# Two token tiles' transposes in a PSUM bank each, emptied in pieces of 128 columns, at the head of a gated attention kernel

## The chip, the cores and the metric

One core of a Trainium2 chip. The metric is the device time of one execution, in microseconds (us). The profiled execution gives a span that is shorter than the time of the same execution (470.1 against 471.88 for the kernel before).

## The reference

Two attention blocks read the same `x` (2048 tokens, 1024 wide) and are mixed by a gate. Only the first projection of block A matters here, the keys:

```python
qkv = (x @ wqkv)...            # A: linear attention; B: sliding, dilated window of 8
q, k, v = qkv[0], qkv[1], qkv[2]
...
x = A_x
g = sigmoid((x * gate_w).sum(-1, keepdims=True))
return g * A(x) + (1 - g) * B(x)
```

## The kernel before

TensorE multiplies `x` by the key weights with `x` transposed: the kernel hands it both operands with the contraction over the 1024 columns along partitions. Most of `x` is transposed by DMA. That path is slow to start: the first such transfer is issued at 1.83 us and lands at 7.31, where the first plain rows, issued at 0.80, land at 3.81. So the first 256 columns (K-slices 0 and 1, of 128 columns each) of token tiles 0 to 3 come in as plain rows, and TensorE transposes them itself into PSUM, the memory that its results go to. PSUM is cut into banks; each tile of the two pools below is one bank.

```python
with tc.manual_schedule(engines={SP, mybir.EngineType.Activation}):
    for kt in range(2):                                   # key weights, slices 0 and 1, 128 KB each
        nc.scalar.dma_start(out=WkA[0][:, kt, :], in_=A_wqkv[kt * P:(kt + 1) * P, D:D + 512])
    load_wk(nc.scalar, 0, 1)                              # slices 0 and 1 of the other half, 256 KB
    load_rows(nc.sync, 0, 2, 0, 2 * P)                    # rows of tiles 0 and 1, 128 KB
    load_rows(nc.sync, 2, 4, 0, 2 * P)                    # rows of tiles 2 and 3
    load_xT(1, 0, 4)                                      # from here on transposed by DMA
    load_wk(nc.sync, 1, 0)
    ...
# ps_pj and ps_1: two PSUM pools of four banks each
def project(pj, t, kt, half):
    nc.tensor.matmul(pj[:], lhsT=xT[:, kt, t * P:(t + 1) * P], rhs=WkA[half][:, kt, :],
                     start=(kt == 0), stop=(kt == KT - 1))

warm_up(26)                                               # 26 matmuls of ones, results unused
def transpose_rows(t):
    for kt in range(2):
        xt = ps_1.tile([P, 2 * P], BF16, name="xt_ps", tag="p1")       # one bank, two tiles
        for i in range(2):
            nc.tensor.transpose(xt[:, i * P:(i + 1) * P], xrow[:, t + i, kt * P:(kt + 1) * P], ident)
        (nc.scalar.copy if kt else nc.vector.tensor_copy)(out=xT[:, kt, t * P:(t + 2) * P], in_=xt[:])

transpose_rows(0)
first = [bank_k(i) for i in range(4)]
for t in range(2):
    project(first[t], t, 0, 0)
transpose_rows(2)
first += [bank_k(i) for i in range(4, 8)]
for t in range(2):
    project(first[t], t, 1, 0)
for half, ts in ((0, (2, 3)), (1, range(4))):
    ...                                                   # then TensorE runs on without a break
```

In the profile a transpose writes `xt_ps`, a copy reads it into `xT`, and a projection writes `pk_ps`.

The softmax here doesn't subtract the row's maximum and nothing guards it: scores larger than these inputs give would overflow.

## Time and profile before

| | kernel before |
|---|---|
| time, median of 3 runs | 472.62 us (472.1 to 472.7) |
| TensorE busy | 466.2 of 470.1 us |
| rows of tile 0 landed | 3.81 us |
| first projection starts | 4.60 us |

The prediction shows the lines behind this table. In them "[0.27 <-DVE xT L211]" means that the engine sat idle for 0.27 us, until the VectorE copy of line 211 let it go. PE is the stream of matmuls and PEld that of weight loads, which run ahead of the matmuls (the load at 4.83 us is for the matmul at 5.04). The ends of matmuls in a profile are modelled, not measured. Idle time of PEld is therefore no loss by itself.

### The profile page before, as it was taken

Reading aid. Unit: us, or ns where it says so; the run is one execution under the profiler, and the core shown is the slowest. Engines: PE = TensorE matmul, PEld = TensorE weight load, DVE = VectorE, ACT = ScalarE, POOL = GpSimd, SP = SyncE. Lnnn points to the kernel's source line nnn. Section 1 sums busy time; section 2 is a strip of 40 time slices with the busy share of each in tenths; the row PEclk is TensorE's granted clock in tenths of the full one; section 3 lists DMA queues with packets and bytes.
Section 4 is the critical chain, followed back from the end, with each engine's and each line's share of the span. In section 5 each row is a group of like instructions: output and inputs, shape, how many; then the busy total and the mean of one; then the engine's idle time right before and its main releaser. Section 6 shows DMA issues by size and latency. Waiting matters only on the chain.

```text
span 470.1 us, 13202 instructions
## 1 busy us (share of the span) xinstructions
PE 466.2 (99%) x5762; PEld 265.9 (57%) x5762; DVE 278.1 (59%) x612; ACT 169.6 (36%) x277; POOL 15.7 (3%) x30
## 2 busy tenths in 40 slices
PE   8999999999999999999999999999999999999997
PEld 5444444445444444444888888888764444444444
DVE  2586689990219999999566676667660049800000
ACT  1443311112433333335465555555543134221121
POOL 2500001400000000000000000000000000000000
PEclk9999999999999999999999999999999999999999
DMA  9999960000653233627326523533763923221111
GB/s 235 201 244 371 349 212 0 0 1 1 226 130 117 83 141 123 162 93 251 105 55 106 116 59 73 88 80 82 92 165 76 216 75 79 68 56 45 34 33 46
DMA packets 98188, 55.14 MB, mean 117 GB/s; under 512 B 69074, under 2 KB 90578, under 8 KB 98130
## 3 DMA queue, kind: packets, MB, share of 16 engines
q1 hardware_dynamic: 92818, 49.61, 41.3%
q10 hardware_dynamic: 5312, 4.69, 3.1%
q8 instruction: 45, 0.74, 0.7%
q14 instruction: 13, 0.11, 0.1%
HBM read 26.10 MB, written 15.86 MB: 89 GB/s over the span
## 4 chain that ended last, share of the span: by engine, by line
PE 99%; DMA 1%; DVE 0%; issue 0%; DVEq 0%
PE q_ps L421 26%; PE d_ps L627 12%; PE p_ps L325 12%; PE pk_ps L196 12%; PE g_ps L264 12%; PE e_ps L627 12%; PE p_ps L361 9%; PE po L501 2%; PE s2b L479 2%; DMA xrow<-in_A_x_dram 1%; PE kv_ps L284 0%; PE w_ps L180 0%; PE xt_ps L210 0%; DVE osb L634 0%; DVE xT L211 0%
## 5 line engine op out<-in xcount | busy, mean ns | idle before, releaser
L421 PE MATMUL q_ps<-xT,WqB 64*64 64x512 bf16 x1024 | 70.2, 376 | 0.0
L421 PE MATMUL q_ps<-xT,WkB 64*64 64x512 bf16 x1024 | 69.8, 376 | 0.0
L171 DVE TENSOR_SCALAR e<-e 128x512 f32<-128x512 f32 x64 | 27.2, 424 | 62.0 <-ACT e L170 61.9
L325 PE MATMUL p_ps<-WvB,xT 128*128 128x512 bf16 x256 | 57.4, 379 | 0.0
L196 PE MATMUL pk_ps<-WkA,xT 128*128 128x512 bf16 x256 | 55.6, 379 | 0.3 <-DVE xT L211 0.3
L264 PE MATMUL g_ps<-pk,xrow 128*128 128x512 bf16 x256 | 55.4, 379 | 0.0
L484 ACT ACTIVATE PT<-s2b 128x928 bf16<-128x928 f32 (+4 forms) x40 | 34.2, 855 | 50.2 <-PE s2b L479 49.2
L486 DVE TENSOR_TENSOR PT<-PT,mask 128x928 bf16<-128x928 bf16 (+4 forms) x40 | 23.6, 589 | 36.5 <-ACT PT L484 36.5
L421 PEld LDWEIGHTS <-WkB 64*64 64x64 bf16 x1024 | 39.7, 107 | 7.3 <-DMA vd<-tmp 0.2
L361 PE MATMUL p_ps<-WqA,xT 128*128 128x512 bf16 x192 | 43.4, 379 | 0.0
L627 PEld LDWEIGHTS <-pqT 128*128 128x128 bf16 x272 | 26.0, 98 | 29.6 <-issue 0.2
L627 PEld LDWEIGHTS <-OBT 128*128 128x128 bf16 x272 | 26.0, 98 | 29.4
L264 PEld LDWEIGHTS <-xrow 128*128 128x128 bf16 x256 | 25.0, 98 | 30.2
L421 PEld LDWEIGHTS <-WqB 64*64 64x64 bf16 x1024 | 38.6, 107 | 6.1 <-DVE qz L461 0.2
L196 PEld LDWEIGHTS <-xT 128*128 128x128 bf16 x256 | 24.8, 98 | 30.3 <-DVE xT L211 0.8
L325 PEld LDWEIGHTS <-xT 128*128 128x128 bf16 x256 | 24.9, 98 | 30.2 <-issue 0.5
L634 DVE TENSOR_SCALAR osb<-e_ps,omg 128x128 bf16<-128x128 f32 x1 | 0.4, 351 | 57.3 <-PE e_ps L627 57.3
L330 ACT CAST tmp<-p_ps 128x512 bf16<-128x512 f32 x32 | 18.7, 587 | 37.9 <-PE p_ps L325 32.5
L501 PEld LDWEIGHTS <-PT 64*56 64x56 bf16 (+2 forms) x1152 | 29.1, 104 | 5.5
L170 ACT ACTIVATE e<-pk_ps 128x512 f32<-128x512 f32 x32 | 18.9, 597 | 36.2 <-PE pk_ps L196 32.5
L361 PEld LDWEIGHTS <-xT 128*128 128x128 bf16 x192 | 18.8, 98 | 22.7
L627 PE MATMUL d_ps<-WoA,pqT 128*128 128x512 bf16 (+1 forms) x136 | 30.9, 370 | 0.0
(71 smaller groups left out, 542.1 us busy)
## 6 DMA issues: line engine op xcount, KB each, us to landing
vd<-tmp SPq DMA_DIRECT2D x16, 264.0 KB
out_dram<-osb ACTq DMA_DIRECT2D x31, 128.0 KB
xrow<-in_A_x_dram SPq DMA_DIRECT2D x3, 1024.0 KB
pqd<-tmp SPq DMA_DIRECT2D x12, 256.0 KB
WvA<-in_A_wqkv_dram SPq DMA_DIRECT2D x2, 1024.0 KB
WoA<-in_A_wo_dram SPq DMA_DIRECT2D x2, 1024.0 KB
WvB<-in_B_wqkv_dram SPq DMA_DIRECT2D x2, 1024.0 KB
WqA<-in_A_wqkv_dram SPq DMA_DIRECT2D x2, 1024.0 KB
```

Of the source, the lines that this page charges most:

```text
L170: nc.scalar.activation(out=e[:], in_=pj[:], func=ACT.Exp)
L171: nc.vector.tensor_scalar(out=e[:], in0=e[:], scalar1=1.0, scalar2=1e-6, op0=ALU.min, op1=ALU.add)
L196: nc.tensor.matmul(pj[:], lhsT=xT[:, kt, t * P:(t + 1) * P], rhs=WkA[half][:, kt, :], start=(kt == 0), stop=(kt == KT - 1))
L264: nc.tensor.matmul(pj[:], lhsT=xrow[:, t, kt * P:(kt + 1) * P], rhs=pk[:, t, half * 512:(half + 1) * 512], start=(t == 0), stop=(t == NB - 1))
L325: nc.tensor.matmul(st["pj"][:], lhsT=xT[:, kt, t * P:(t + 1) * P], rhs=WvB[half][:, kt, :], start=(kt == 0), stop=(kt == KT - 1))
L330: nc.scalar.copy(out=v[:, half * 16:(half + 1) * 16, 0:Dh], in_=st["pj"][:].rearrange("p (h e) -> p h e", h=16))
L361: nc.tensor.matmul(st["pj"][:], lhsT=xT[:, kt, t * P:(t + 1) * P], rhs=WqA[half][:, kt, :], start=(kt == 0), stop=(kt == KT - 1))
L421: nc.tensor.matmul(banks[o][64 * j:64 * j + 64, :], lhsT=lhsT(r, kt, j), rhs=rhs(r, kt), start=first and kt == 0, stop=kt == KT - 1, skip_ ...
L484: nc.scalar.activation(out=pt[:, :, 0:W_], in_=s2b[:].rearrange("p a b s -> p (a b) s")[:, :, 0:W_], func=ACT.Exp, scale=SCALE)
L486: nc.vector.tensor_tensor(out=pt[:, :, 0:W_], in0=pt[:, :, 0:W_], in1=mask[:, None, base:base + W_].broadcast_to([P, 4, W_]), op=ALU.mult)
L501: nc.tensor.matmul(o2[64 * h:64 * h + w, par, s_, i, :], lhsT=pt[r, i, o:o + w], rhs=V[r, m, 4 * c + i, :], start=True, stop=True)
L627: nc.tensor.matmul(st["ps"][:, 0:n], lhsT=lhsT, rhs=W[c0 // 512][:, c, c0 % 512:c0 % 512 + n], start=(side == 0 and c == 0), stop=(side == ...
```

## The change

Its intent is to let the first projection start earlier. The copy that releases it should wait for one transpose instead of two, and carry 128 columns instead of 256. To use what the pieces bring first, both K-slices of tile 0 are projected, then the next transposes are made, then tile 1 is projected.

```diff
-            def transpose_rows(t):
+            def transpose_rows(t, n):
                 for kt in range(2):
-                    xt = ps_1.tile([P, 2 * P], BF16, name="xt_ps", tag="p1")
-                    for i in range(2):
+                    xt = ps_1.tile([P, n * P], BF16, name="xt_ps", tag="p1")
+                    for i in range(n):
                         nc.tensor.transpose(xt[:, i * P:(i + 1) * P], xrow[:, t + i, kt * P:(kt + 1) * P], ident)
-                    (nc.scalar.copy if kt else nc.vector.tensor_copy)(out=xT[:, kt, t * P:(t + 2) * P], in_=xt[:])
+                    (nc.scalar.copy if kt else nc.vector.tensor_copy)(out=xT[:, kt, t * P:(t + n) * P], in_=xt[:])
...
-            transpose_rows(0)
+            transpose_rows(0, 1)
+            transpose_rows(1, 1)
             first = [bank_k(i) for i in range(4)]
-            for t in range(2):
-                project(first[t], t, 0, 0)
-            transpose_rows(2)
+            for kt in range(2):
+                project(first[0], 0, kt, 0)
+            transpose_rows(2, 2)
             first += [bank_k(i) for i in range(4, 8)]
-            for t in range(2):
-                project(first[t], t, 1, 0)
+            for kt in range(2):
+                project(first[1], 1, kt, 0)
```

## The prediction

> **What bounds the kernel now.** I read the page's busy table first, then the chain that ended last, then that chain in order of time for the first 9 us, then the timeline of the same stretch, because the diff touches nothing later than the first eight tile transposes.
>
> ```profile
> span 470.1 us, 13202 instructions
> ...
> PE 466.2 (99%) x5762; PEld 265.9 (57%) x5762; DVE 278.1 (59%) x612; ACT 169.6 (36%) x277; POOL 15.7 (3%) x30
> ...
> PE 99%; DMA 1%; DVE 0%; issue 0%; DVEq 0%
> ```
>
> TensorE is busy in 466.2 of 470.1 us and carries the chain. All engines together leave 3.9 us in which it is not busy, so a change that only removes waits of TensorE cannot gain 2% (9.4 us). The chain in order of time says where the part before the steady stream lies:
>
> ```profile
> 0.80 3.01 DMA xrow<-in_A_x_dram
> 3.81 0.05 issue
> 3.86 0.37 PE xt_ps L210 x2
> 4.23 0.02 issue
> 4.25 0.30 DVE xT L211
> 4.55 0.05 issue
> 4.60 0.60 PE pk_ps L196 x2
> 5.20 0.22 PE xt_ps L210 x4
> 5.43 3.69 PE pk_ps L196 x17
> ```
>
> The reader is to see one hop off TensorE: the rows of x arrive at 3.81, two transposes are made, VectorE copies them to SBUF, and only then does the first projection start, at 4.60. That hop is what the change shortens. The timeline of the stretch (start, duration, engine, instruction, idle time before it) gives the sizes:
>
> ```profile
> 3.86 0.47 PE L210 MATMUL xt_ps<-pk,xrow 128*128 128x128 bf16 x4
> 4.25 0.29 DVE L211 COPY xT<-xt_ps 128x256 bf16<-128x256 bf16 x1 [0.80 <-PE xt_ps L210]
> 4.36 2.14 SPq L95 DMA_TRANSPOSE xT<-in_A_x_dram  x1
> 4.36 0.37 ACT L211 COPY xT<-xt_ps 128x256 bf16<-128x256 bf16 x1 [2.28 <-PE xt_ps L210]
> 4.59 0.11 PEld L196 LDWEIGHTS <-xT 128*128 128x128 bf16 x2 [0.44 <-DVE xT L211]
> 4.60 0.60 PE L196 MATMUL pk_ps<-WkA,xT 128*128 128x512 bf16 x2 [0.27 <-DVE xT L211]
> ...
> 5.35 0.29 DVE L211 COPY xT<-xt_ps 128x256 bf16<-128x256 bf16 x1 [0.81 <-PE xt_ps L210]
> 5.46 0.37 ACT L211 COPY xT<-xt_ps 128x256 bf16<-128x256 bf16 x1 [0.73 <-PE xt_ps L210]
> 5.70 10.26 PEld L196 LDWEIGHTS <-xT 128*128 128x128 bf16 x49 [0.34 <-DVE xT L211]
> ```
>
> TensorE sits idle for 0.27 us before the first projection, the only idle time it has there after the rows landed. The 0.34 us ahead of 5.70 is idle time of the weight loads, which run ahead of the matmuls; the matmuls show no gap there.
>
> Reading the trace instruction by instruction, in ns precision: the four transposes start at 3.858, 3.938, 4.045 and 4.105 and last 0.288, 0.274, 0.223 and 0.219; the VectorE copy starts at 4.250 (0.038 after the end of transpose two), the ScalarE copy at 4.361 (0.037 after the end of transpose four); the copy ends at 4.540, the weight load follows at 4.593 (0.053 later), its matmul at 4.598. Full-width projections then start 0.216 apart. The landing records give: first rows 3.811, second rows 4.614, the four 128-KB and 256-KB pieces of the K weights in order of use 3.543, 4.211, 6.288 and 8.023. A weight load that waited for rows started 0.042 after the landing.
>
> **What the Trainium skill says.** "PSUM — Partial Sum Buffer", section "PSUM bank collisions raise a hardware error": semaphores must guard PSUM by bank and quadrant, not by address. That is why two transposes that share a bank must both be finished before an engine reads either, and why the change needs a bank for each. The trace agrees in that no copy starts before the second transpose of its bank has ended (4.250 against 4.212). "VectorE: DVE Perf Modes", section "Why PSUM operands drop a tier": a bf16 copy out of PSUM gets at most two results per cycle, at the stated 0.96 GHz 0.52 ns per column. The copy of 256 columns took 0.291 us; no bf16 copy of another width is in this trace, so slope and fixed part cannot be separated from it alone, and I take the page's. "ScalarE: Activation LUTs", section "What ACT_TABLE_LOAD costs": 0.833 ns per element; the trace has 0.587 us at 512 and 0.372 at 256 columns, 0.84 ns per column, so it agrees. "TensorE: Matmul & The Clock Gate", section "Single matmul latency": 289 ns cold and 219 ns warm for 128 columns by its formulas; the first transpose took 288, the fourth 219, so the array changes speed inside these four transposes. This depends on time and not on the order of instructions.
>
> **The change part by part.** Comparing the two instruction streams with the line numbers taken off, only the head differs: VectorE and ScalarE each get one copy more (two of 128 columns in place of one of 256), TensorE has the same number of instructions with two projections swapped, and the DMA queues are unchanged. Before, the four transposes went K-slice 0 of tiles 0 and 1, then slice 1 of both; now they go both slices of tile 0, then both of tile 1, so the second and the third swap. Their sizes and starting times stay. ("First copy" below is VectorE's, of slice 0.)
>
> 1. First copy starts earlier: transpose one ends at 3.858 + 0.288 = 4.146, plus 0.038 gives 4.184 instead of 4.250. Gain 0.066.
> 2. First copy is shorter: 128 columns fewer at 0.52 ns is 0.067, so 0.291 becomes about 0.225, and it ends at 4.409 instead of 4.540. Steps 1 and 2 together: 0.13.
> 3. Weight load at 4.409 + 0.053 = 4.462, first projection at about 4.468 instead of 4.598. Gain on the path 0.13.
> 4. The second projection now needs the ScalarE copy of tile 0. It starts at 4.212 + 0.037 = 4.249, lasts 0.372 - 128 x 0.84 ns = 0.265, ends at 4.514; weight load possible at 4.567. The matmul would go at 4.468 + 0.226 = 4.694, so 0.13 us is to spare. Its K weights landed at 4.211. No wait.
> 5. The next transposes move from 5.040 to 4.91; the load for them moves from 4.826 to 4.696, against rows usable at 4.614 + 0.042 = 4.656. It passes with 0.04 to spare. Their banks were emptied by then (4.409 and 4.514).
> 6. Tile 1: VectorE's second copy from about 4.41 to 4.64, ScalarE's from 4.51 to 4.78, both needed at about 5.13. Hidden. One copy more on each engine adds about 0.16 us of fixed time to VectorE and to ScalarE, off the path.
> 7. Tiles 2 and 3: in both kernels 0.606 us from the sixth transpose to the projection that uses it, so they move with it. The other half of the weights: needed at 6.575 - 0.13 = 6.445, landed 6.288. The second slice pair: needed at 8.302 - 0.13 = 8.172, usable at 8.023 + 0.042 = 8.065. Passes with 0.1 to spare.
>
> Sum: 0.13 us off the start of the stream. After 5.3 us I searched all intervals between matmul starts for those over 0.228 us; nine are left, of 0.23 to 0.32 us, all next to a change of phase, and all would move with the stream. So the 0.13 us should reach the end: 472.62 - 0.13 = 472.49.
>
> **The rivals.** (a) A DMA takes the place of the copy. If rows or weights came 0.1 us later in another run, steps 5 and 7 would wait and give back part or all of the 0.13. For it: the margins are 0.04 and 0.1, and TensorE starts 0.04 after the first landing, so DMA sets this stretch already. Against it: the change issues no transfer differently. It makes 472.5 to 472.62. (b) ScalarE becomes the bound. The swap puts its copy, formerly needed only at 5.21, directly behind the first projection. If a short ScalarE copy has not 0.265 but over 0.39 us, or starts only after transpose three, the second projection waits. The 128x128 activation from PSUM with a scale took 0.367, which would still just fit. It makes at worst 472.6. (c) The fixed part dominates: if VectorE's 128-column copy takes 0.28 (the two-input 128x128 operation in the attention took 0.285), only step 1 remains, 472.55. If instead the copy ran at one column per cycle, it gains 0.2 us, 472.42. (d) The array's clock steps up at another moment in another run, as the warm-up is timed by a window. A later step costs each affected 512-column matmul about 0.2 us (an estimate: four times the 0.107 less 0.056 us between starts of 128-column ones before and after the step in this trace), for either kernel; this is scatter, larger than the effect. Favoured: the full 0.13, then (a).
>
> **Range and chances.** The three runs of before scatter over 0.6 us (472.1 to 472.7), nearly five times the effect. Median 472.5; with the scatter and a possible offset between chips I give 471.7 to 473.2. For 2% either way there would have to be 9.4 us; the head in question lasts 0.8 us. Chances: faster 0.005, within 2% 0.99, slower 0.005.
>
> **What would show it.** Right: a first VectorE copy of 128x128 near 4.18 lasting 0.22 to 0.23, a first projection near 4.47, TensorE idle before it 0.14 instead of 0.27, the ScalarE copy near 4.25 lasting 0.26 to 0.27 with no gap before the second projection, and TensorE unbroken from there. Times count from the landing of the rows, should it not be at 3.81. Wrong: a wait of a weight load or matmul for rows or K weights at 4.7, 6.4 or 8.1 (rival a); a gap before the second projection released by ScalarE (b); a copy over 0.27 (c); an unchanged time in which the first projection is early but a later matmul waits.

## The result, and the profile after

The changed kernel took 472.12 us (median of 6 runs, 471.73 to 472.63), the kernel before 472.33 us in its 6 runs. The ratio is 0.9999, with a 95% interval of 0.9986 to 1.0012: the same. A ratio here is the mean time of one kernel's fast runs over that of the other's of the same rounds, so it is not quite the ratio of the medians.

The profile of the changed kernel, the chain that ended last in order of time (start, duration, what):

```profile
0.80 3.04 DMA xrow<-in_A_x_dram
3.84 0.05 issue
3.88 0.61 PE xt_ps L210 x4
4.49 1.03 PE pk_ps L196 x2
5.53 0.43 PE xt_ps L210 x4
5.95 3.24 PE pk_ps L196 x13
```

The first projection starts at 4.49 instead of 4.60, although the rows landed 0.03 later. But two projections take 1.03 us here where they took 0.60, and this profile's span is longer, 470.9 against 470.1 us. Its timeline:

```profile
3.88 0.61 PE L210 MATMUL xt_ps<-pk,xrow 128*128 128x128 bf16 x4
4.21 0.44 DVE L211 COPY xT<-xt_ps 128x128 bf16<-128x128 bf16 x2 [0.76 <-PE xt_ps L210]
4.32 0.48 ACT L211 COPY xT<-xt_ps 128x128 bf16<-128x128 bf16 x2 [2.23 <-PE xt_ps L210]
4.49 0.25 PEld L196 LDWEIGHTS <-xT 128*128 128x128 bf16 x2 [0.26 <-DVE xT L211]
4.49 1.03 PE L196 MATMUL pk_ps<-WkA,xT 128*128 128x512 bf16 x2
```

The VectorE copy is no longer in the chain, but only because the modelled end of the fourth transpose (4.493 us) reaches just past the projection's start (4.491). The first projection still hangs on that copy: it ends at 4.435, and the weight load that waits for it starts 0.052 later, as it started 0.053 later before.

The copies are what was predicted: 0.224 us each on VectorE (predicted 0.225) and 0.266 on ScalarE (0.265). What differs is TensorE. Its transposes start 0.107 us apart and its 512-column projections 0.427 apart, twice the 0.056 and 0.216 of the full clock. The trace's own clock record puts the start of the full clock at 6.707 us in this execution and at 4.043 us in the profile of before. Was that the change, or chance? The page's row of granted clock does not tell: it shows 9, that is full, in every slice of both kernels, the first ones too. The half rate is to be read from the distances of the matmuls.

### The profile page after: what moved, and what is told of

The parts are those of the page before. It is cut to its first block, busy times and chain, and to the rows that moved or that the text cites. A ratio compares the mean times of both kernels' runs of the same rounds, so it can differ in the third digit from the quotient of the medians.

```text
span 470.9 us, 13174 instructions
## 1 busy us (share of the span) xinstructions
PE 465.6 (99%) x5732; PEld 269.6 (57%) x5762; DVE 278.2 (59%) x613; ACT 169.8 (36%) x278; POOL 15.4 (3%) x30
## 4 chain that ended last, share of the span: by engine, by line
PE 98%; DMA 1%; issue 0%; DVE 0%; DVEq 0%
PE q_ps L422 26%; PE d_ps L628 12%; PE pk_ps L196 12%; PE g_ps L265 12%; PE p_ps L326 12%; PE e_ps L628 11%; PE p_ps L362 9%; PE po L502 2%; PE s2b L480 2%; DMA xrow<-in_A_x_dram 1%; PE kv_ps L285 0%; PE w_ps L180 0%; PE xt_ps L210 0%; DVE osb L635 0%; DVEq L635 0%
```

## The experiments

Theory 1: the hop is shorter by about what was predicted, and the moment of the clock step is chance. Theory 2: the change itself delays the step, and so eats its gain. Theory 3: the gain is given back to a later wait. The 95% interval of the result is 1.2 us wide and the predicted gain was 0.13 us, so times cannot decide between these. I used three means: repeated profiles, a head run 20 times over, and a shorter warm-up.

### The two kernels again

`before_again` and `after_again` are the unchanged kernels.

> Unchanged kernel before, for its scatter. Theory 1 (the start of the full array clock is a matter of chance in each run and explains the scatter): the step from 0.107 to 0.056 us between 128-column matmul starts (0.43 to 0.216 us for 512 columns) falls anywhere from about 4 to 7.5 us, so this profile's step may differ from the 4.0 us of the first profile; the span follows it by about half a microsecond per microsecond. Theory 2 (the scatter comes from elsewhere, DMA say): the step falls near 4.0 us again in every profile of this kernel. Runs between 471.6 and 472.8 under both.

> Unchanged changed kernel, a second look. From the end of the row landing to the first projection: 0.65 us (it was 0.653 in the first profile), against 0.79 in the kernel before, whatever the clock. Theory 1: the step to the full clock lies elsewhere than the 6.6 us of the first profile. Theory 2: it is again at 6.6 us, that is, the change itself delays it. Time within 0.1% of the kernel before under theory 1; up to 0.8 us slower at equal landing under theory 2.

Measured: 472.09 us (5 runs) and 472.05 us (5 runs), against 472.37 us for 9 runs of the kernel before. The clock stepped up at 5.599 and 5.622 us. The same kernel before had 4.043 the first time and the changed one 6.707, so the moment is not fixed by either kernel, and theory 2 falls as a fixed delay (two more profiles of the changed kernel follow below; with so few, a small shift of the average could hide). By luck this pair has equal steps and nearly equal landings (3.644 and 3.651), so it can be compared directly. Timelines, first the kernel before, then the changed one:

```profile
4.12 0.29 DVE L211 COPY xT<-xt_ps 128x256 bf16<-128x256 bf16 x1 [0.67 <-PE xt_ps L210]
4.47 1.03 PE L196 MATMUL pk_ps<-WkA,xT 128*128 128x512 bf16 x2 [0.17 <-DVE xT L211]
```

```profile
4.02 0.44 DVE L211 COPY xT<-xt_ps 128x128 bf16<-128x128 bf16 x2 [0.57 <-PE xt_ps L210]
4.30 1.03 PE L196 MATMUL pk_ps<-WkA,xT 128*128 128x512 bf16 x2
```

The reader is to see the idle time that the profile shows for TensorE, 0.17 us, gone. At ns precision the first projection starts 0.781 us after the first transpose before, and 0.607 after: 0.174 less. The second set of transposes starts 1.609 and 1.433 after it: 0.176 less. So nothing is given back at the second projection, which follows the first by 0.401 and 0.399 us.

Yet from the first transpose to the start of the kernel's last matmul it is 463.680 us before and 463.627 after, only 0.053 less. Two things took the rest. The step comes at a fixed moment. An engine that gets to work 0.176 us earlier at half rate has done, by the step, what takes 0.088 us at full rate; the gain is halved. And a weight piece landed at 6.892 us in this run (6.27 in the first profile of the changed kernel); a projection that would have followed its forerunner by 0.216 us followed by 0.260, a stall of 0.044. The two leave 0.044 of 0.176, near the 0.053 measured. The traces show where it goes: counted from the first transpose, the changed kernel is ahead by 0.085 us at the fourth projection, just after the step, by 0.052 at the ninth, which waited for the weights, and by 0.053 at the last matmul. So theory 1 holds, and theory 3 in part.

### The head run 20 times

To multiply the cost of one hop, `x20_before` and `x20_after` run the eight transposes, their copies and the four projections 20 times ahead of the real head. The results of these projections are thrown away; the outputs stay correct.

```diff
+            for _ in range(20):
+                transpose_rows(0)                      # x20_after: the changed form of these lines
+                again = [bank_k(0) for i in range(2)]
+                for t in range(2):
+                    project(again[t], t, 0, 0, True)   # True: ends the accumulation after slice 1
+                transpose_rows(2)
+                for t in range(2):
+                    project(again[t], t, 1, 0, True)
             transpose_rows(0)
```

> The head (eight transposes, their copies, four projections) run 20 times more ahead of the real one, in the form of before, so that what one pass costs is multiplied by 20 under a warm clock. Worked out from the durations of the first profile: one pass 1.75 us, so 35 us more than the kernel before (507.5 us). It only serves as the base for the next.

> The same 20 passes in the changed form. Theory A (the prediction): each pass is 0.12 to 0.13 us shorter, 2.4 to 2.6 us in all against the 20 passes of before. Theory B (the gain at the first projection is given back at the second, which now waits for ScalarE, or at the next transposes): under 0.6 us in all. Theory C (more copies and semaphores cost more than they save): slower than the 20 passes of before.

Measured: 507.64 us and 505.33 us (4 runs each), 2.31 us apart. Theory A holds, B and C fall. In the traces a pass at full clock takes 1.758 us before and 1.635 after, 0.123 less (from the first transpose of a pass to that of the next). One pass before, then one after:

```profile
26.01 0.39 PE L210 MATMUL xt_ps<-pk,xrow 128*128 128x128 bf16 x4
...
26.33 0.29 DVE L211 COPY xT<-xt_ps 128x256 bf16<-128x256 bf16 x1 [0.36 <-PE xt_ps L210]
...
26.68 0.60 PE L196 MATMUL pk_ps<-WkA,xT 128*128 128x512 bf16 x2 [0.27 <-DVE xT L211]
```

```profile
26.23 0.46 PE L210 MATMUL xt_ps<-pk,xrow 128*128 128x128 bf16 x4
26.48 0.36 DVE L211 COPY xT<-xt_ps 128x128 bf16<-128x128 bf16 x2 [0.31 <-PE xt_ps L210]
...
26.76 0.60 PE L196 MATMUL pk_ps<-WkA,xT 128*128 128x512 bf16 x2
```

From the start of the transposes to the copy it is 0.312 us before and 0.256 after (0.056 less, the distance of two transposes at full clock). The copy is 0.067 shorter. The sum is 0.123, the whole difference. Twenty times that is 2.46 us; the 2.31 us of the medians agree within their scatter (the 4 runs of each kernel spread over about 1.5 us).

### Which part of the change does it

Three more kernels of 20 passes take the parts one by one.

`x20_pieces`: the bank stays shared, only the copy of tiles 0 and 1 is cut. Tile 1 is transposed first, so that the copy of tile 0 waits for both and never reads a bank that is being written (diff against `x20_before`).

```diff
-                    for i in range(2):
+                    for i in (1, 0):
                         nc.tensor.transpose(...)
-                    (...)(out=xT[:, kt, t * P:(t + 2) * P], in_=xt[:])
+                    for i, n in ((0, 1), (1, 1)) if t == 0 else ((0, 2),):
+                        (...)(out=xT[:, kt, (t + i) * P:(t + i + n) * P], in_=xt[:, i * P:(i + n) * P])
```

> 20 passes with only the shorter copy: the two tiles still share a bank, tile 1 is transposed first, so that the copy of tile 0 waits for both as before, but it is taken alone, in 128 columns. Projections in the order of before. By the prediction's two terms (0.066 earlier, 0.067 shorter; the profiles show 0.056 between the ends of two transposes under a warm clock): a pass 0.066 us shorter than 1.758, so 1.69, 1.3 us in all against the 20 passes of before. If the length of the copy did not count (only the bank): 0. If the bank did not count: 2.3, as with the full change.

`x20_split_oldorder`: banks and pieces of the change, projections in the order of before (diff against `x20_after`).

```diff
             transpose_rows(0, 1)
             transpose_rows(1, 1)
             first = [bank_k(i) for i in range(4)]
-            for kt in range(2):
-                project(first[0], 0, kt, 0)            # and so on, also in the passes
+            for t in range(2):
+                project(first[t], t, 0, 0)
```

> 20 passes with a bank for each transpose and copies of 128 columns, but the projections in the order of before (slice 0 of tiles 0 and 1, next transposes, slice 1 of both). If the gain is wholly the bank and the piece: 1.635 us a pass as in the full change (2.3 us in all less than the 20 passes of before); the second projection then hangs on VectorE's second copy, with nothing to spare by the durations. If the new order of the projections is what lets the split pay: less, down to half of it.

`x20_pairs_neworder`: pairs and 256-column copies of before, projections in the new order (diff against `x20_before`).

```diff
             transpose_rows(0)
             first = [bank_k(i) for i in range(4)]
-            for t in range(2):
-                project(first[t], t, 0, 0)             # and so on, also in the passes
+            for kt in range(2):
+                project(first[0], 0, kt, 0)
```

> 20 passes with the pairs of before (a bank and a copy of 256 columns for two transposes), but both rows of tile 0 first, then the next transposes. If the order alone is worth nothing: 1.758 us a pass, within 0.1 us of the 20 passes of before in all. If the order gains by itself: under 1.72. If it costs (ScalarE's 0.372-us copy holds the second projection): over 1.78.

| | median us (4 runs) | one pass at full clock, from the trace |
|---|---|---|
| x20_before | 507.64 | 1.758 |
| x20_pieces | 506.28 | 1.692 |
| x20_split_oldorder | 505.43 | 1.636 |
| x20_pairs_neworder | 508.41 | 1.787 |
| x20_after | 505.33 | 1.635 |

(The middle three ran in another call; the kernel before had 472.37 us in the first call and 472.19 in the second.)

In the timeline of a pass of `x20_pieces` the copy starts 0.31 us after the transposes, as before, but is short:

```profile
26.38 0.39 PE L210 MATMUL xt_ps<-pk,xrow 128*128 128x128 bf16 x4
26.69 0.36 DVE L212 COPY xT<-xt_ps 128x128 bf16<-128x128 bf16 x2 [0.36 <-PE xt_ps L210]
...
26.97 0.61 PE L196 MATMUL pk_ps<-WkA,xT 128*128 128x512 bf16 x2 [0.21 <-DVE xT L212]
```

The shorter copy alone is worth 0.066 us a pass, a bank for each transpose another 0.056, and the order of the projections nothing beside the split. The 0.056 is the worth of waiting for one transpose instead of two. That a bank of its own is needed for this is the prediction's reading of the skill; no run copies from a bank that TensorE is still writing, so it is not tested here. The order without the split cost 0.029 us a pass, the branch of the expectation in which ScalarE's copy holds the second projection. The timeline of a pass shows who holds the second projection's weights:

```profile
26.28 0.37 ACT L211 COPY xT<-xt_ps 128x256 bf16<-128x256 bf16 x1 [0.28 <-PE xt_ps L210]
...
26.70 0.10 PEld L196 LDWEIGHTS <-xT 128*128 128x128 bf16 x1 [0.15 <-ACT xT L211]
```

That is the prediction's rival (b), ScalarE as the bound. Part of it is made by the repetition: a copy in the repeated passes also waits for its own earlier copy into the same place, and ScalarE starts it 0.092 us after the transposes end, where it took 0.037 in the single head. By these 0.055 us, more than the 0.029 lost, a single head should escape the wait; that is argued, not shown, as I did not run the new order alone in one.

### A shorter warm-up

`short_warm` is the changed kernel with `warm_up(2)` in place of `warm_up(26)`.

> The changed kernel with 2 warm-up matmuls in place of 26, so that the array's busy time begins at 3.8 us and not at 0.8. If the step to the full clock follows from a window of busy time that starts at chance: the step falls between about 7 and 10.7 us, some 3 us later, and as half of that time is lost, the kernel is about 1.5 us slower than the changed kernel (473.6), with the same scatter. If the step has nothing to do with the warm-up: 472.1. The first projection stays 0.65 us after the landing of the rows.

Measured: 473.60 us (4 runs, 473.33 to 474.1), against 472.19 for 7 runs of the kernel before, 0.28% slower by the ratio; the clock stepped up at 9.477 us. The timeline shows the half-rate stretch in the weight loads, which come one at a time until 9.36:

```profile
3.66 0.61 PE L210 MATMUL xt_ps<-pk,xrow 128*128 128x128 bf16 x4 [2.45 <-DMA xrow<-in_A_x_dram]
...
8.93 0.15 PEld L196 LDWEIGHTS <-xT 128*128 128x128 bf16 x1 [0.28 <-issue]
9.36 2.53 PEld L196 LDWEIGHTS <-xT 128*128 128x128 bf16 x12 [0.28 <-issue]
```

The first projection stands 0.655 us after the landing, as in the changed kernel. So the warm-up's length moves the step, and the step moves the time. This is also what the Trainium skill says ("TensorE: Matmul & The Clock Gate", section "What's actually happening"): full rate is granted after a busy window of 3413 ns, and the windows run free of the kernel's start. The clock records agree: the stretches at full clock last 467.626 us in two profiles without the repeated head (`before` and `rows_first`, below) and 464.213 in six, 137 and 136 times 3.4133. One thing fits less well: in the first profile of before the step came 3.20 us after the first warm-up matmul, a little less than a window. Either a window need not be busy from end to end, or work ahead of the kernel counted; no run here tells.

### Tile 0's rows first

The hop begins with the landing of the rows, so a version that lands them earlier might beat both kernels. `after_third` and `after_fourth` are the changed kernel once more, as partners.

```diff
-        load_rows(nc.sync, 0, 2, 0, 2 * P)
-        load_rows(nc.sync, 2, 4, 0, 2 * P)
+        load_rows(nc.sync, 0, 1, 0, 2 * P)
+        load_rows(nc.sync, 1, 2, 0, 2 * P)
+        # rows_first:  load_rows(nc.scalar, 2, 4, ...) ahead of load_wk(nc.scalar, 0, 1)
+        # rows_first2: load_rows(nc.sync, 2, 4, ...) here
-            warm_up(26)
+            warm_up(23)
```

> The changed kernel a third time, as the partner of the next run on the same chip and as one more look at scatter. First projection 0.65 us after the landing of tile 0's rows if the array is still at half rate by then, about 0.63 if it is not; the step to the full clock anywhere from 4 to 7.5 us; median 471.9 to 472.4.

> The changed kernel, with the rows of tile 0 loaded by a DMA of their own (64 KB), then those of tile 1, and those of tiles 2 and 3 on the ScalarE queue after the two first weight pieces; 23 warm-up matmuls, so that they end before. If what sets the landing is the number of bytes ahead: 64 KB less at the 270 to 290 GB/s of that stretch is about 0.2 us, tile 0's rows land near 3.5 instead of 3.65 to 3.84, and the first projection is 0.2 us earlier; what follows is then limited by tile 1's rows or by the second weight piece (4.06 to 4.25 so far), so about 0.1 to 0.2 us of gain. If latency or the weight traffic sets it: landing unchanged, no gain, or a loss where the rows of tiles 2 and 3 come later than 4.6. Not to be seen in the times (scatter 0.9 us), only in the trace.

Measured: 472.43 us (6 runs) and 474.65 us (6 runs), with 472.29 for the kernel before. The step of `after_third` was at 6.722 us, and its first projection 0.656 us after the landing. In `rows_first` tile 0's rows landed at 3.128, better than the 3.5 expected, and the first projection started at 4.09. Then the kernel lost far more than that. Waits for DMA from its timeline:

```profile
5.10 0.40 PE L211 MATMUL xt_ps<-pk,xrow 128*128 128x128 bf16 x4 [0.41 <-DMA xrow<-in_A_x_dram]
...
8.71 11.60 PE L197 MATMUL pk_ps<-WkA,xT 128*128 128x512 bf16 x52 [1.90 <-DMA WkA<-in_A_wqkv_dram]
```

One transfer more was in flight. The weight piece behind it on the ScalarE queue waited on the semaphore of tile 0's rows, was issued at 3.149 instead of 1.75 us and landed at 8.665, where it landed at 6.877 in its partner `after_third`.

> The changed kernel again, as partner of the next run on the same chip. First projection 0.61 us after the first transpose at half rate, about 0.65 after the landing; 471.8 to 472.5.

> As the run with tile 0's rows loaded first, but with the order of the other transfers mended: in the last one the piece of weights on the ScalarE queue was the ninth transfer, whose issue waited for the first to land, and it came 2.3 us late (8.665 against 6.27 to 6.33). Now all three row transfers go ahead on the SyncE queue and the weights on the ScalarE queue go as in the changed kernel. Tile 0's rows near 3.13 again, tile 1's near 3.5, the first transpose at about 3.5 (held by the identity matrix that VectorE builds until 3.45), first projection near 4.1 instead of 4.27 to 4.49; the rows of tiles 2 and 3 at 4.4 to 4.6 as before, so the gain is 0.15 to 0.3 us if no later piece holds TensorE, and about 0.1 if the weights that landed at 6.27 to 6.33 do. If the earlier transfers shift the later ones by their 0.45 us of issue: a stall of 0.2 to 0.5 us near 8 us, and no gain or a loss.

Measured: 472.07 us (5 runs) and 474.65 us (6 runs), with 471.89 for the kernel before. The mend failed too: tile 0's rows came at 3.127 and the first projection started at 4.092, but the rows of tiles 2 and 3, now the third transfer on the SyncE queue, landed at 6.659, not at the 4.4 to 4.6 that I expected:

```profile
6.71 0.61 PE L211 MATMUL xt_ps<-pk,xrow 128*128 128x128 bf16 x4 [1.58 <-DMA xrow<-in_A_x_dram]
```

The same bytes landed at 5.054 as the third transfer on the ScalarE queue in `rows_first`. Why the third on the SyncE queue took so long is open. No version beat the two kernels.

`after_fourth` is instructive by itself, as its step came early (between the first and second projection: this trace has no clock record, but they start 0.331 us apart, neither the 0.401 of half rate nor the 0.226 of full). With the array fast, the DMAs become the limit:

```profile
4.90 0.23 PEld L210 LDWEIGHTS <-xrow 128*128 128x128 bf16 x4 [0.35 <-DMA xrow<-in_A_x_dram]
4.90 0.40 PE L210 MATMUL xt_ps<-pk,xrow 128*128 128x128 bf16 x4
...
6.58 1.39 PEld L196 LDWEIGHTS <-xT 128*128 128x128 bf16 x7 [0.25 <-issue]
```

Tile 2's rows landed at 4.859, and the transpose that would have started 0.216 us after the second projection started 0.269 after it, 0.053 late. The next weight piece landed at 6.542, and its projection started at 6.584, 0.135 late. Together these stalls are 0.188 us, more than the hop's gain.

## Why the prediction was right or wrong

The time lay in the range, and "the same" was right. Over all, 22 runs of the changed kernel have a mean of 472.36 us and 39 of the kernel before 472.23; the standard errors (standard deviation over the root of the number of runs) are 0.11 and 0.06. The changed kernel is 0.12 us higher, about one standard error of the difference, so even these runs show no gain of 0.13 us. What can be judged is the working.

- **Steps 1 and 2** held in mechanism and nearly in size. The shorter copy is worth 0.067 us, as predicted. The earlier start is worth 0.056 at full clock and 0.109 at half (the copy starts 0.433 and 0.324 us after the first transpose in the matched pair); the 0.066 came from a profile in which the step fell among the four transposes. The prediction took the step to depend on time, not on the order of instructions; the two profiles of the unchanged kernel, with steps at 4.043 and 5.599 us, bear that out. But it then kept the starting times of this one profile for every run. Its remark that the trace agrees with the skill on the shared bank shows little, since a copy of 256 columns needs both transposes in any case.
- **Step 3**: from the landing of the rows to the first projection, 0.787 became 0.653 between the first two profiles, 0.134 as predicted. But the clock differed between them. With equal clocks it is 0.174 at half rate and 0.123 at full rate. The idle time of 0.14 us that I expected to remain is not shown at half rate, where the modelled end of the fourth transpose covers it; the projection waits for the copy all the same.
- **Steps 4 and 6** held. No single-head profile has a wait for ScalarE, and the extra copies were hidden.
- **Steps 5 and 7** failed in some runs. I took landing times from one profile as if fixed. The rows of tiles 2 and 3 landed between 4.400 and 4.859 us and the next weights between 6.266 and 6.892 in the six single-head profiles with the full warm-up. My margins were 0.04 and about 0.1. That is rival (a), seen in two of four profiles of the changed kernel.
- **The sum**, "so the 0.13 us should reach the end", is the step that failed. The search for gaps was right, but of the two limits at the head I treated one (clock) as scatter and the other (DMA) as a margin. At half rate up to a fixed step the gain counts half; with an early step the DMA can take it, as in `after_fourth`. In the one matched pair 0.053 us reached the end.
- **Rival (d)** was named as scatter larger than the effect. The changed kernel's profiles bear it out: between `after` and `after_third` the step comes 0.238 us later relative to the first transpose, and the rest of the kernel is 0.118 us longer, half of it. With `short_warm` the step is another 2.758 us later and the rest 1.482 longer, 0.54 of it. At that rate steps between 4.0 and 6.7 us, as seen here, would move the time by over 1 us (an estimate: half of 2.7), as much as the scatter of most runs. The most that two profiles of the changed kernel with 26 warm-up matmuls differ in it is 0.87 us (463.276 in `after_fourth`, 464.149 in `after_third`, from the first transpose to the last matmul). Three runs of 473.04, 473.27 and 473.91 lie outside that, and what slowed them is not known.

## What to carry to other kernels

A hop between engines shortens by what its first consumer needs: give that piece a bank and a copy of its own, and here the two gave 0.056 and 0.067 us a pass at full clock. Before counting such a gain at the end, ask what sets the time after it, since here a gain made while the array was still at half rate counted about half, and a transfer with a margin of 0.1 us took more of it in some runs. Where an effect is smaller than the scatter, run the part many times over inside one kernel, and compare traces of equal clock.

## What the Trainium skill lacked or had wrong

- "TensorE: Matmul & The Clock Gate", "Part 4: PE-mode transpose", says that the full clock does not engage for transposes and that one took about 275 ns in a kernel. Here transposes ran at the full rate once the array had stepped up: 219 ns each, starts 0.056 us apart.
- The same page, "Single matmul latency": the half-rate formula gives 289 and 609 ns for a single matmul of 128 and 512 columns, and the first of a series took 289 and 608. For those behind it the page has no figure: the profiles show 314 and 634, 25 ns more (their ends are modelled).
- No page that I read gives the cost of a second semaphore in a wait. ScalarE started its copy 0.037 us after the transposes' end with one; with two, of which it waited for the transposes first and for its own earlier copy second, it took 0.092. VectorE, which in the same passes waited for the transposes last, took 0.037 with two. So the order of the waits seems to matter; no run tests it.
- No page that I read tells how late a transfer lands behind others on its queue. The rows of tiles 2 and 3 as third transfer on the SyncE queue landed at 6.659 us, the same bytes as third on the ScalarE queue at 5.054.
